# Retention attention and two dense layers on one core: other token blocks for the first layer, another order of the norms in the second

## The chip, the cores and the metric

The program runs on one core of one Trainium2 chip. A core has a matrix engine (TensorE, PE in the profile, with its weight loads shown apart as PEld), a vector engine (VectorE, DVE), a scalar engine (ScalarE, ACT), GpSimd (POOL) and a queue engine that issues the transfers (SyncE, SP). Each engine takes its instructions strictly in the order in which the program lists them, and waits on semaphores where it needs another engine's result. The metric is the device time of one execution in microseconds (us); lower is better.

## What is computed

```python
# attention: q, k, v of (4, 8, 576, 64)
ret = (scale * q @ k.T) * Dmat            # Dmat: gamma**(i-j) below the diagonal, 0 above
x = (ret @ v) -> (2304, 512)              # 2304 tokens, 512 features
# first layer: w_in (512, 2048), w_out (2048, 512)
h = x @ w_in
x = (h * sigmoid(1.702 * h)) @ w_out
# second layer: w_in (512, 1024), w_out (1024, 512)
h = x @ w_in
e = exp(h - max(h)); solu = h * e / (sum(e) + 1e-9)
ln = (solu - mean(solu)) / sqrt(var(solu) + 1e-6) * g_ln
out = ln @ w_out
```

## The kernel before

**Precision.** A float32 product is made of three matmuls on halves: each operand is split into a high part (a rounding copy, cast on ACT or DVE) and a low part (the difference, on POOL or DVE), and the products high-high, low-high and high-low are summed in PSUM. So every logical matmul is three instructions, each with its own weight load.

**First layer.** The 2304 tokens are cut into five blocks (`BLOCKS`): four of 464 tokens and one of 448. The 16 column groups of `w_in` are taken in three generations (`GENS`) of 3, 5 and 8 groups, since the split weights don't all fit. `STEPS` runs over generation, block and group: 80 steps. A step issues 12 matmuls for h (`emit_h`, L442; moving operand as wide as the block) and 12 matmuls for the step before it that add into y (`emit_y`, L472). Between them stands a chain: a sigmoid on ACT (L447), a product on DVE (L448), a cast (L452 on DVE or L450 on ACT) and a subtraction on DVE (L453). `split_x` makes the halves of the next block's x near the end of a block (ACT L422, POOL L423), in pieces that don't cross a sequence's end (every 576 tokens). At a block's end y is copied by ACT (L478, first generation) or added by DVE (L480). In between, `background` slips in pieces of weight preparation (conversions on DVE, L225 to L236; splits on ACT L248 and POOL L253), a set number for each step.

**Second layer.** Its 18 tiles of 128 tokens are taken in 9 pairs. For a pair p, `split_y` makes seven split operands (subtractions on DVE, casts on ACT L507, subtractions on POOL L508). `emit_h2(p)` computes the two tiles' h by a scheme with seven products instead of eight: the products are made in the order B, A, C, A, B, C, D, each of six matmuls (L546), with adds on DVE (L552) and copies on ACT (L555, L558, L564) between them; the fifth product writes over the bank of the first, so it waits for the first add (c12) to have read it. `hooks` are places in `emit_h2` where the caller puts other work into the order.

`norm(t, steps)` is the work on tile t: step 1 is a maximum on DVE (L583) and an exponential on ACT (L584); step 2 is a product u*e on DVE (L586, alone as "u") and then the statistics ("v": L588 to L593 on DVE and a power of one column on POOL, L594); step 3 is the scaling on DVE (L596). `turn(t)` transposes the tile on PE (`emit_T`, L607), and splits the result (ACT L616, DVE L617); it needs step 3. `out(t)` multiplies by `w_out` (L634, 24 matmuls), copies the result (ACT L639) and stores it (SP). After pair 1 the order for a pair is: `emit_h2(p+1)`, `turn(2p)`, `split_y(p+2)`, maxima and exponentials of the new pair, `out(2p-1)`, step 2, `turn(2p+1)`, step 2, `out(2p)`.

Of the kernel before, what the change touches and what calls it, by code (L numbers as in the profile page):

```python
# [10 lines left out]
F32R = mybir.dt.float32r  # L11
# [8 lines left out]
NT = B * S  # L20
DM = H * D
F1 = 2048
F2 = 1024
P = 128
CH = 128
NCH = 4
LAST = S - NCH * CH
TB = 464
NB = -(-NT // TB)
BLOCKS = [(t, min(TB, NT - t)) for t in range(0, NT, TB)]  # L30
NF = F1 // P
FH = NF // 2
GENS = ((0, 3), (3, 8), (8, 16))
# [86 lines left out]
RAW_AT = [_M["att"], _M["att"] + SLICE]  # L120
T_LATER = T_START + [SCAN_AT] + [_M["att"] + (2 + i) * SLICE for i in range(5)]
# [3 lines left out]
E_AT = [RAW_AT[1], T_LATER[4]]  # L125
# [1 line left out]
IDENT_AT = _M["g"]  # L127
STAT_AT = IDENT_AT + P
S_AT = [T_LATER[4], T_LATER[5], T_LATER[4]] + [T_LATER[5]] * 6
E_FIRST = RAW_AT[0]  # L130

# [13 lines left out]
class Build:  # L147
    def __init__(self, tc, ctx, att, consts, ident_in, w1, w2in, w2out, out):
        self.tc, self.nc = tc, tc.nc
        self.att_in, self.const_in, self.ident_in = att, consts, ident_in  # L150
        self.w1_in, self.w2in_in, self.w2out_in, self.out = w1, w2in, w2out, out
        pool = lambda name: ctx.enter_context(tc.tile_pool(name=name, bufs=1))
        self.mem = pool("mem").tile([P, CMEM], F32, name="mem")
        self.wp = pool("wp")
        self.ctx, self.early, self.early_s = ctx, ExitStack(), ExitStack()
        pad = ctx.enter_context(tc.tile_pool(name="pad", bufs=1, side="right"))
        self.pad = pad.tile([P, RIGHT_PAD], F32, name="pad")
        self.gs = self.early_s.enter_context(
            tc.tile_pool(name="gsp", bufs=1, side="right", reuse_waits="tile")
        ).tile([P, 4, 512], F32R, name="gs")  # L160
        self.xp = self.early.enter_context(tc.tile_pool(name="xp", bufs=1, reuse_waits="tile"))
        self.xsp = self.early_s.enter_context(
            tc.tile_pool(name="xsp", bufs=1, side="right", reuse_waits="tile")
        )
        self.xb = self.xp.tile([P, B * NP * S], F32, name="xb")
        self.xst, self.w, self.wraw = {}, {}, {}
        self.ps = ctx.enter_context(tc.tile_pool(name="ps", bufs=1, space=bass.MemoryType.PSUM))
        self.bg, self.split, self.staged = [], set(), set()
# [242 lines left out]
    def split_x(self, gen, j, k):  # L411

        nc = self.nc
        t = self.xsp.tile([P, 2, 512], F32R, tag="xs", name=f"xs{gen}_{j}_{k}", bufs=6)
        self.xst[gen, j, k] = t
        (t0, width), done = BLOCKS[j], 0
        while done < width:
            b, s = divmod(t0 + done, S)
            n = min(width - done, S - s)
            assert (4, b * NP + k) in self.staged  # L420
            x = self.x(b * NP + k)[:, s:s + n]
            nc.scalar.copy(t[:, 0, done:done + n], x)  # L422
            nc.gpsimd.tensor_tensor(  # L423
                t[:, 1, done:done + n], x, f32(t[:, 0, done:done + n]), ALU.subtract
            )
            done += n
# [4 lines left out]
    def emit_h(self, gen, j, f, lo_engine, hi_act=False):  # L431
# [12 lines left out]
        b = BUF[gen, j, f]  # L444
        g = self.at(_M["g"] + b * TB, width)
        gs = self.gs[:, b * 2:b * 2 + 2, 0:width]
# [82 lines left out]
    def emit_h2(self, p, hooks={}):  # L529

        nc = self.nc
        ys = self.xst.pop(p)

        B_, A, C, D_ = (self.ybank(f"h2_{p}_{i}") for i in range(4))
        c11, c12, c21, c22 = (
            self.h(2 * p + i)[:, n * 512:(n + 1) * 512] for i in range(2) for n in range(2)
        )

        def mul(o, a, b, start, stop):
            a = ys[a]  # L540
            i = 0
            hi, lo = self.w[b]
            for k in range(2):
                w = slice(k * 512, (k + 1) * 512)
                for l, m in ((0, hi), (1, hi), (0, lo)):
                    nc.tensor.matmul(  # L546
                        o, a[:, l, k], m[:, w], start=(start and i == 0), stop=(stop and i == 5),
                        skip_group_check=True,
                    )
                    i += 1  # L550

        add = lambda o, a, b: nc.vector.tensor_tensor(o, a, b, ALU.add)  # L552
        mul(B_, "s2", "t2", True, True)
        mul(A, "a11", "b11", True, True)
        nc.scalar.copy(c11, A)  # L555
        add(c12, B_, c11)
        mul(C, "s1", "t1", True, True)
        nc.scalar.copy(c22, C)  # L558
        hooks.get("u2", int)()
        mul(A, "a12", "b21", False, True)  # L560
        mul(B_, "s3", "t3", False, True)
        mul(C, "s4", "b22", False, True)
        add(c21, B_, c11)
        nc.scalar.copy(c11, A)  # L564
        add(c22, c22, c21)
        add(c12, C, c12)
        hooks.get("p3", int)()
        hooks.get("c12", int)()
        mul(D_, "a22", "t4", True, True)
        add(c21, D_, c21)  # L570

    def norm(self, t, *steps):

        nc = self.nc
        u, e = self.h(t), self.at(E_FIRST if t == 1 else E_AT[t % 2], F2)
        st = self.at(STAT_AT + (t % 4) * 32, 32)
        nm, sm, q, v, r = (st[:, i:i + 1] for i in range(5))
        bn = st[:, 6:18].rearrange("r (n s) -> r n s", n=2)  # L580
        mv = st[:, 18:20]
        if 1 in steps:
            nc.vector.reduce_max(nm, u, axis=AX.X, negate=True)  # L583
            nc.scalar.activation(e, u, AF.Exp, bias=nm, accum_out=sm)  # L584
        if 2 in steps or "u" in steps:
            nc.vector.tensor_tensor(u, u, e, ALU.mult)  # L586
        if 2 in steps or "v" in steps:
            nc.vector.tensor_scalar_add(q, sm, 1e-9)  # L588
            nc.vector.tensor_scalar(q, q, q, 1e-6, ALU.mult, ALU.mult)  # L589
            for n in range(2):  # L590
                nc.vector.bn_stats(bn[:, n], u[:, n * 512:(n + 1) * 512])  # L591
            nc.vector.bn_aggr(mv, bn)  # L592
            nc.vector.tensor_tensor(v, mv[:, 1:2], q, ALU.add)  # L593
            nc.gpsimd.tensor_tensor(r, v, self.const("half"), ALU.pow)  # L594
        if 3 in steps:
            nc.vector.tensor_scalar(u, u, mv[:, 0:1], r, ALU.subtract, ALU.mult)  # L596
# [46 lines left out]
    def run(self):  # L643
# [35 lines left out]
        for f in range(FH):  # L679
            t = T_START[f % 2]  # L680
# [7 lines left out]
        last = B * NP - 1  # L688
# [36 lines left out]
        for g, j, f in STEPS:  # L725
            fl, n = f - GENS[g][0], GENS[g][1] - GENS[g][0]
            start = g == 0 and j == 0
# [42 lines left out]
            if g == len(GENS) - 1 and last_block:  # L770
                assert not self.bg
                if fl == 0:
                    self.open_second()
                    ys, y1, y2 = (self.split_y(p) for p in range(3))
# [22 lines left out]
        def turn(t):  # L797
            zs[t] = self.split_z(t, self.emit_T(t))

        def out(t):  # L800
            self.emit_out(t, zs.pop(t))


        last = [
            self.split_weight(NF + i, T_LATER[4 + i], pool) for i, pool in ((2, None), (3, (self.zsp, 1)))
        ]
        def run(pieces):
            for piece in pieces:
                piece()
# [3 lines left out]
        nc.scalar.activation(self.at(STAT_AT, 1), self.const("half"), AF.Exp)  # L813

        self.emit_h2(0, {
            "u2": lambda: run(y1[6:8] + last[1]), "p3": lambda: run(y1[8:]), "c12": lambda: self.norm(0, 1),
        })

        def first():
            self.norm(0, "v")  # L820
            self.norm(0, 3)
            self.norm(1, 1)

        def start():
            turn(0)
            run(y2[4:])
            self.norm(1, 2)

        self.norm(0, "u")
        self.emit_h2(1, {"u2": first, "p3": start})  # L830
        self.norm(1, 3)
        self.norm(2, 1)
        out(0)
        turn(1)
        pairs = NTT // 2
        for p in range(1, pairs):
            more = p + 1 < pairs
            if p == 1:
                self.emit_h2(p + 1, {"u2": lambda: [self.norm(2, 2), self.norm(3, 1), self.norm(2, 3)]})
            elif more:  # L840
                self.emit_h2(p + 1, {"u2": lambda: [self.norm(2 * p + i, 3) for i in range(2)]})
            else:
                self.norm(2 * p, 3)
                self.norm(2 * p + 1, 2, 3)
            turn(2 * p)
            if p == 1:
                self.norm(3, 2, 3)
            if p + 2 < pairs:
                run(self.split_y(p + 2))
            if more:  # L850
                self.norm(2 * p + 2, 1)
                self.norm(2 * p + 3, 1)
            out(2 * p - 1)
            if more:
                self.norm(2 * p + 2, 2)
            turn(2 * p + 1)
            if p + 2 < pairs:
                self.norm(2 * p + 3, 2)
            out(2 * p)
        out(NTT - 1)  # L860
# [74 lines left out]
```

## Time and profile before

| | |
|---|---|
| median of three timed runs | 686.6 us (686.52 to 687.75) |
| the profiled execution's own time | 684.85 us |
| its span, first to last instruction | 683.1 us |
| mean granted TensorE clock | 0.999 |
| busy: PE, DVE, ACT, POOL | 670.5, 491.7, 234.4, 232.0 us |

The rows are of the profiled execution, so sums are made against its 684.85 us, which is 1.75 us over its span and 1.75 us below the median. In the rows, times are from the start of the span. "x12" means that twelve instructions of one kind in a row are merged in a line; the first number is the start of the first of them. What stands in brackets is the idle time of the engine before the line, and what ended it.

### The profile page before, as it was taken

How to read it: one execution, taken by the hardware profiler on the slowest of the kernel's cores; microseconds unless marked ns; L12 is line 12 of the kernel's file. 1: busy time of each engine (PE TensorE's matmuls, PEld its weight loads, DVE VectorE, ACT ScalarE, POOL GpSimd, SP SyncE). 2: the span in 40 equal slices, each digit the busy share in tenths (PEclk: the TensorE clock that was granted, in tenths of full speed). 3: DMA queues.
4: the chain of work that ended last, by engine and by line, in shares of the span. 5: the costliest groups of instructions: out<-in, count | busy, mean ns of one | idle time of the engine just before them, and what ended most of it. 6: DMA issues, size and time to landing. Idle time of an engine off the chain costs nothing. (4 is left out here: it accounts for less than half of the span.)

```text
span 683.1 us, 10367 instructions
## 1 busy us (share of the span) xinstructions
PE 670.5 (98%) x4070; PEld 591.5 (87%) x4070; DVE 491.7 (72%) x805; ACT 234.4 (34%) x483; POOL 232.0 (34%) x240
## 2 busy tenths in 40 slices
PE   8999999999999999999999999999989999999998
PEld 7999888998888899988888888998777788888887
DVE  3899766877887876577676775565779877877780
ACT  3654444442112134111111211456535424453331
POOL 1211366453323248411120301396634314431300
PEclk9999999999999999999999999999999999999999
DMA  8999400002213110012211100000000000000001
GB/s 326 422 383 373 155 0 2 0 1 94 92 63 124 61 62 1 0 63 93 92 63 62 63 1 0 1 1 4 1 15 32 1 31 32 31 17 17 31 32 47
DMA packets 13441, 49.34 MB, mean 72 GB/s; under 512 B 1488, under 2 KB 2384, under 8 KB 11984
## 3 DMA queue, kind: packets, MB, share of 16 engines
q1 hardware_dynamic: 13392, 48.68, 19.5%
q8 instruction: 32, 0.52, 0.3%
q14 instruction: 17, 0.14, 0.1%
HBM read 43.95 MB, written 4.72 MB: 71 GB/s over the span
## 5 line engine op out<-in xcount | busy, mean ns | idle before, releaser
L442 PE MATMUL h<-xs,w 128*128 128x464 f32 (+1 forms) x960 | 213.4, 371 | 0.4 <-POOL xs L423 0.4
L472 PE MATMUL yp<-gs,w 128*128 128x464 f32 (+1 forms) x960 | 212.2, 370 | 0.0
L442 PEld LDWEIGHTS h<-xs,w 128*128 128x128 f32 x960 | 180.1, 188 | 21.0 <-POOL xs L423 2.0
L472 PEld LDWEIGHTS yp<-gs,w 128*128 128x128 f32 x960 | 180.3, 188 | 18.9
L423 POOL TENSOR_TENSOR xs<-xb,xs 128x112 fp32r<-128x112 f32 (+4 forms) x96 | 92.7, 993 | 227.6 <-ACT xs L422 227.6
L447 ACT ACTIVATE mem<-h 128x464 f32<-128x464 f32 (+1 forms) x80 | 44.6, 557 | 263.9 <-PE h L442 246.1
L448 DVE TENSOR_TENSOR mem<-h,mem 128x464 f32<-128x464 f32 (+1 forms) x80 | 51.0, 638 | 95.0 <-ACT mem L447 94.7
L634 PE MATMUL o<-w,zs 128*128 128x512 f32 (+1 forms) x456 | 103.2, 382 | 1.2 <-ACT zs L616 0.9
L634 PEld LDWEIGHTS o<-w,zs 128*128 128x128 f32 x456 | 81.2, 188 | 17.0 <-ACT zs L616 1.4
L253 POOL TENSOR_TENSOR w<-mem,w 128x512 fp32r<-128x512 f32 x40 | 54.2, 1383 | 68.3 <-ACT w L248 68.3
L453 DVE TENSOR_TENSOR gs<-mem,gs 128x464 fp32r<-128x464 f32 (+1 forms) x80 | 66.5, 831 | 13.6 <-ACT gs L450 7.0
L508 POOL TENSOR_TENSOR ys_s<-mem,ys_s 128x256 fp32r<-128x256 f32 x36 | 33.8, 950 | 58.4 <-ACT ys_s L507 58.4
L452 DVE CAST gs<-mem 128x464 fp32r<-128x464 f32 (+1 forms) x69 | 42.0, 608 | 6.6
L546 PE MATMUL h<-wt,ys_s 128*128 128x512 f32 x162 | 41.4, 391 | 0.7 <-DVE mem L552 0.7
L552 DVE TENSOR_TENSOR mem<-h,mem 128x512 f32<-128x512 f32 x36 | 24.7, 687 | 22.1 <-PE h L546 13.5
L546 PEld LDWEIGHTS h<-wt,ys_s 128*128 128x128 f32 x162 | 30.3, 188 | 7.3 <-DVE mem L552 1.2
L422 ACT CAST xs<-xb 128x112 fp32r<-128x112 f32 (+4 forms) x96 | 34.9, 431 | 0.0
L594 POOL TENSOR_TENSOR mem<-mem 128x1 f32<-128x1 f32 x18 | 9.9, 551 | 65.2 <-DVE mem L593 65.2
L617 DVE TENSOR_TENSOR zs<-zT,zs 128x512 fp32r<-128x512 f32 x36 | 23.1, 685 | 9.3 <-ACT zs L616 9.3
L586 DVE TENSOR_TENSOR mem<-mem 128x1024 f32<-128x1024 f32 x18 | 25.4, 1410 | 4.4 <-ACT mem L584 4.4
L546 PE MATMUL h<-wb,ys_a 128*128 128x512 f32 x108 | 27.4, 389 | 0.0
L584 ACT ACTIVATE mem<-mem 128x1024 f32<-128x1024 f32 x18 | 20.6, 1145 | 18.7 <-DVE mem L583 18.7
(80 smaller groups left out, 732.6 us busy)
## 6 DMA issues: line engine op xcount, KB each, us to landing
mem<-in_att SPq DMA_DIRECT2D x11, 1120.0 KB, 8.2
wraw<-in_w SPq DMA_DIRECT2D x16, 512.0 KB, 10.3
mem<-in_w SPq DMA_DIRECT2D x16, 512.0 KB, 3.5
out<-mem SPq DMA_DIRECT2D x17, 256.0 KB, 2.0
mem<-in_w2in SPq DMA_DIRECT2D x8, 512.0 KB, 3.4
mem<-in_w2out SPq DMA_DIRECT2D x8, 512.0 KB, 3.5
mem<-in_att SPq DMA_DIRECT2D x5, 544.0 KB, 8.7
mem<-in_att SPq DMA_DIRECT2D x4, 576.0 KB, 8.7
```

What stands on the lines that cost most here:

```text
L253: nc.gpsimd.tensor_tensor(lo[:, c], w[:, c], f32(hi[:, c]), ALU.subtract)
L422: nc.scalar.copy(t[:, 0, done:done + n], x)
L423: nc.gpsimd.tensor_tensor(t[:, 1, done:done + n], x, f32(t[:, 0, done:done + n]), ALU.subtract)
L442: nc.tensor.matmul(h[:, 0:width], a[:, w], x[:, b, 0:width], start=(n == 0), stop=(n == 3 * KB - 1))
L447: nc.scalar.activation(g, h[:, 0:width], AF.Sigmoid, scale=1.702)
L448: nc.vector.tensor_tensor(g, h[:, 0:width], g, ALU.mult)
L452: nc.vector.tensor_copy(gs[:, 0], g)
L453: lo_engine.tensor_tensor(gs[:, 1], g, f32(gs[:, 0]), ALU.subtract)
L472: nc.tensor.matmul(o, a[:, w], gs[:, b], start=(first and i == 0), stop=(last and i == 2))
L508: nc.gpsimd.tensor_tensor(ys[:, 1], src, f32(ys[:, 0]), ALU.subtract)
L546: nc.tensor.matmul(o, a[:, l, k], m[:, w], start=(start and i == 0), stop=(stop and i == 5), skip_group_check=True,)
L634: nc.tensor.matmul(o[:, 0:n], z[:, a, k], b[:, c:c + n], start=(k == 0 and i == 0), stop=(k == FB - 1 and i == 2),)
```

## The change

The five blocks of the first layer become 384, 512, 512, 512 and 384 tokens wide; the buffers that were `TB` wide follow. The number of blocks, steps and matmuls stays. In the second layer, the maximum and the exponential of a tile can now be issued apart ("max", "exp"), `emit_h2` has two more hook places (`c21`, right after the second add, and `sums`, after the last of the middle adds; `p3` now stands before these adds), and for the tiles 0 to 5 the steps are issued in another order. Tile 3's exponential gets a buffer of its own (`E_FIRST`).

```diff
-TB = 464
-NB = -(-NT // TB)
-BLOCKS = [(t, min(TB, NT - t)) for t in range(0, NT, TB)]
+TB = 512
+WIDTHS = (384, 512, 512, 512, 384)
+NB = len(WIDTHS)
+BLOCKS = [(sum(WIDTHS[:j]), w) for j, w in enumerate(WIDTHS)]
...
-E_FIRST = RAW_AT[0]
+E_FIRST = {1: RAW_AT[0], 3: T_LATER[5]}
...
         mul(C, "s4", "b22", False, True)
+        hooks.get("p3", int)()
         add(c21, B_, c11)
+        hooks.get("c21", int)()
         nc.scalar.copy(c11, A)
         add(c22, c22, c21)
         add(c12, C, c12)
-        hooks.get("p3", int)()
+        hooks.get("sums", int)()
         hooks.get("c12", int)()
...
-        if 1 in steps:
+        if 1 in steps or "max" in steps:
             nc.vector.reduce_max(nm, u, axis=AX.X, negate=True)
+        if 1 in steps or "exp" in steps:
             nc.scalar.activation(e, u, AF.Exp, bias=nm, accum_out=sm)
...
-            "u2": lambda: run(y1[6:8] + last[1]), "p3": lambda: run(y1[8:]), "c12": lambda: self.norm(0, 1),
+            "u2": lambda: run(y1[6:8] + last[1]), "sums": lambda: run(y1[8:]), "c12": lambda: self.norm(0, 1),
...
         def first():
-            self.norm(0, "v")
-            self.norm(0, 3)
-            self.norm(1, 1)
+            self.norm(1, "exp")
+            self.norm(0, "v", 3)
+            self.norm(1, "u")
 
         def start():
             turn(0)
+            self.norm(1, "v")
             run(y2[4:])
-            self.norm(1, 2)
-
+
+        self.norm(1, "max")
         self.norm(0, "u")
-        self.emit_h2(1, {"u2": first, "p3": start})
-        self.norm(1, 3)
+        self.emit_h2(1, {"u2": first, "p3": start, "c21": lambda: self.norm(1, 3)})
         self.norm(2, 1)
+        self.norm(3, "max")
         out(0)
         turn(1)
...
             if p == 1:
-                self.emit_h2(p + 1, {"u2": lambda: [self.norm(2, 2), self.norm(3, 1), self.norm(2, 3)]})
+                self.emit_h2(p + 1, {
+                    "u2": lambda: [self.norm(3, "exp"), self.norm(2, 2)],
+                    "c21": lambda: [self.norm(2, 3), self.norm(3, 2)], "sums": lambda: self.norm(3, 3),
+                })
+            elif p == 2:
+                self.emit_h2(p + 1, {"u2": lambda: [self.norm(4, 3), self.norm(5, 2, 3)]})
...
             turn(2 * p)
-            if p == 1:
-                self.norm(3, 2, 3)
...
             turn(2 * p + 1)
-            if p + 2 < pairs:
+            if 1 < p < pairs - 2:
                 self.norm(2 * p + 3, 2)
```

## Rows read from the trace of the kernel before

**Rows 1.** The page's busy times: us, share of the span, instructions.
```profile
PE 670.5 (98%) x4070; PEld 591.5 (87%) x4070; DVE 491.7 (72%) x805; ACT 234.4 (34%) x483; POOL 232.0 (34%) x240
```

**Rows 2.** Groups by line and shape, TensorE: busy us, mean ns of one.
```profile
L442 PE MATMUL h<-xs,w 128*128 128x464 f32 x768 | 171.9, 372 | 0.4 <-POOL xs L423 0.4
...
L442 PE MATMUL h<-xs,w 128*128 128x448 f32 x192 | 41.5, 365 | 0.0
```

**Rows 3.** Timeline of the first layer: start, us, engine, line; PE groups of h.
```profile
325.64 2.67 PE L442 MATMUL h<-xs,w 128*128 128x464 f32 x12
...
345.69 2.67 PE L442 MATMUL h<-xs,w 128*128 128x464 f32 x12
...
441.00 2.59 PE L442 MATMUL h<-xs,w 128*128 128x448 f32 x12
...
462.88 2.60 PE L472 MATMUL yp<-gs,w 128*128 128x448 f32 x12
```

**Rows 4.** The chain that ended last, in order of time: start, us, what.
```profile
594.83 9.52 PE h L546 x42
...
668.71 11.25 PE o L634 x72
```

**Rows 5.** Timeline of the second layer's first pairs, TensorE alone.
```profile
491.20 1.64 PE L546 MATMUL h<-wt,ys_a 128*128 128x512 f32 x6
...
493.77 0.50 PE L634 MATMUL o<-w,zs 128*128 128x512 f32 x1 [0.93 <-ACT zs L616]
...
494.50 5.48 PE L634 MATMUL o<-w,zs 128*128 128x512 f32 x23 [0.22 <-DVE zs L617]
...
501.89 1.09 PE L607 MATMUL zT<-mem 128*128 128x128 f32 x8 [1.91 <-DVE mem L596]
...
513.17 5.73 PE L634 MATMUL o<-w,zs 128*128 128x512 f32 x24
...
520.60 1.06 PE L607 MATMUL zT<-mem 128*128 128x128 f32 x8 [1.70 <-DVE mem L596]
...
526.97 1.52 PE L546 MATMUL h<-wt,ys_s 128*128 128x512 f32 x6
...
533.32 1.66 PE L546 MATMUL h<-wt,ys_s 128*128 128x512 f32 x6 [0.74 <-DVE mem L552]
```

**Rows 6.** The same stretch: VectorE, ScalarE and GpSimd around the norms.
```profile
482.10 1.22 DVE L583 TENSOR_REDUCE mem<-mem 128x1 f32<-128x1024 f32 x1
...
484.62 1.65 DVE L586 TENSOR_TENSOR mem<-mem 128x1024 f32<-128x1024 f32 x1 [0.71 <-ACT mem L584]
...
486.80 0.14 DVE L588 TENSOR_SCALAR mem<-mem 128x1 f32<-128x1 f32 x1
...
489.48 0.81 DVE L596 TENSOR_SCALAR mem<-mem 128x1024 f32<-128x1024 f32 x1 [0.67 <-POOL mem L594]
...
500.43 0.56 POOL L594 TENSOR_TENSOR mem<-mem 128x1 f32<-128x1 f32 x1
...
503.06 1.16 ACT L584 ACTIVATE mem<-mem 128x1024 f32<-128x1024 f32 x1 [6.71 <-DVE mem L583]
...
505.29 1.29 DVE L617 TENSOR_TENSOR zs<-zT,zs 128x512 fp32r<-128x512 f32 x2 [2.33 <-ACT zs L616]
...
532.58 0.68 DVE L552 TENSOR_TENSOR mem<-h,mem 128x512 f32<-128x512 f32 x1
```

**Rows 7.** Timeline of the first layer's last block, VectorE.
```profile
456.10 2.93 DVE L487 TENSOR_TENSOR mem<-mem 128x512 f32<-128x512 f32 x2
...
461.64 0.63 DVE L453 TENSOR_TENSOR gs<-mem,gs 128x448 fp32r<-128x448 f32 x1 [0.64 <-ACT gs L450]
```

**Rows 8.** Timeline of the second block's first step: POOL's splits, PE's wait.
```profile
85.02 2.92 POOL L423 TENSOR_TENSOR xs<-xb,xs 128x112 fp32r<-128x112 f32 x4 [6.48 <-ACT xs L422]
...
87.99 0.48 PE L442 MATMUL h<-xs,w 128*128 128x464 f32 x1 [0.37 <-POOL xs L423]
```

**Rows 9.** Busy time of each engine in one stretch of the first layer.
```profile
170.00:290.00 120.00, 120.00 (x579) 108.37 (x579) 90.80 (x131) 29.86 (x57) 48.52 (x43) 1.00 0.18 57
```

More of the change, by code (lines that the diff above doesn't have):

```diff
@@ L159, in __init__ @@
             tc.tile_pool(name="gsp", bufs=1, side="right", reuse_waits="tile")
-        ).tile([P, 4, 512], F32R, name="gs")
+        ).tile([P, 4, TB], F32R, name="gs")
         self.xp = self.early.enter_context(tc.tile_pool(name="xp", bufs=1, reuse_waits="tile"))
@@ L413, in split_x @@
         nc = self.nc
-        t = self.xsp.tile([P, 2, 512], F32R, tag="xs", name=f"xs{gen}_{j}_{k}", bufs=6)
+        t = self.xsp.tile([P, 2, TB], F32R, tag="xs", name=f"xs{gen}_{j}_{k}", bufs=6)
         self.xst[gen, j, k] = t
@@ L576, in norm @@
         nc = self.nc
-        u, e = self.h(t), self.at(E_FIRST if t == 1 else E_AT[t % 2], F2)
+        u, e = self.h(t), self.at(E_FIRST.get(t, E_AT[t % 2]), F2)
         st = self.at(STAT_AT + (t % 4) * 32, 32)
```

## The prediction

> **What bounds the kernel now.** I read the page's busy times first: PE works through 98% of the span [rows 1], DVE through 72%. So PE sets the time, and only two things can move it: the time from one matmul's start to the next, and PE's idle time. Next came the chain that ended last. From 533 us to the end it holds PE alone, but for the last copy and store (in rows 4 two of its links), so whatever PE gains before that point arrives at the end whole. Then the timeline. In the first layer PE's groups follow one another without idle time, but for rare waits as in rows 8. In the second layer's first pairs five PE groups start late [rows 5]; later pairs show none of it.
>
> How far apart matmuls start is read from the starts of groups, since the mean of one [rows 2] is a latency that overlaps the next. 464 wide: 8 groups of 12 lie between 325.64 and 345.69, so 20.05 / 96 = 208.9 ns. 448 wide: 9 groups between 441.00 and 462.88 give 21.88 / 108 = 202.6 ns [rows 3]. 512 wide: 9.52 / 42 = 226.7 ns [rows 4]. 256 wide: the last 72 matmuls are 24 of 512 and 48 of 256 columns, so (11.25 - 24 x 0.2267) / 48 = 121 ns [rows 4]. The clock is at its upper level, 2.4 GHz (1.00 in rows 9), at which the columns alone take 193.3, 186.7, 213.3 and 106.7 ns. What comes on top is 15.6, 15.9, 13.4 and 14 ns. It isn't the same at all widths: 512 and 256 columns pay about 13.5, 464 and 448 nearly 16.
>
> **The widths.** The first layer has 1536 matmuls of 464 columns and 384 of 448 (rows 2 for h; y has as many): 1536 x 0.2089 + 384 x 0.2026 = 320.9 + 77.8 = 398.7 us. After: 1152 of 512 and 768 of 384. For 512, I take 226.7 ns: it is the same width, though measured in the other layer. 384 isn't in the trace. Its columns take 160.0 ns; from below it adds 13.3 ns (as 512), from above 15.9 (as 448). I take 13.3, so 173.3 ns, since 384 is like 512 and 256 a whole number of 128 columns, which 464 and 448 are not; that this is what counts is a guess. Sum: 261.2 + 133.1 = 394.3, **4.4 us less**. With the upper end for 384 it is 396.3, 2.4 less. With about 15.7 ns for every width nothing changes, as the columns and the number of matmuls stay.
>
> The Trainium skill ("TensorE: Matmul & The Clock Gate", Back-to-back issue gap) gives a warm gap of N / 2.4 + 2.5 ns, an overhead that doesn't know the width. The rows disagree with its size (226.7 where it gives 215.8) and with its being constant; by it, the widths would give nothing.
>
> What the widths may cost. A step of 384 takes 24 x 0.1733 = 4.16 us instead of 5.01, and work that has no width must fit in it.
> - The second block's first h waits 0.37 us for POOL's split of x [rows 8]. The new block is 512 wide: its four pieces take 2.92 x 512/464 = 3.22, 0.3 more, while PE gets there about 0.2 sooner and the chain ahead of the split is as much shorter. +0.3 us.
> - In the last block, all of POOL's weight splits go on at the old pace and stretch DVE: two subtractions of 512 columns take 2.93 us [rows 7] where such an add takes 0.68 [rows 6]. There the low half of g is ready at 461.64 + 0.63 = 462.27 for a y group at 462.88 [rows 3]: 0.6 us to spare. The time from the end of h to that y group is one step's, and shrinks by 24 x (0.2026 - 0.1733) = 0.7, the DVE chain itself by 0.1 to 0.2 at most, so part of the step waits, and the next one may. I take +0.7 us for this block.
> - DVE as a whole: 90.80 of 120 us [rows 9], 3.8 us in a step of 5.01. Even if none of it shrank it would fit in 4.16.
> Together **+1.0 us**, from 0.2 to 2.5. The number of x pieces stays (8 for each generation and quarter of x, before and after), and no transfer is added or moved past another.
>
> **The norms.** What PE loses now, by starts [rows 5] and 226.7 ns for a matmul: 491.20 + 6 x 0.2267 = 492.56 to 493.77, 1.21; 494.00 to 494.50, 0.50; 494.50 + 23 x 0.2267 = 499.71 to 501.89, 2.18; 513.17 + 24 x 0.2267 = 518.61 to 520.60, 1.99; 526.97 + 24 x 0.2267 = 532.41 to 533.32, 0.91. Sum 6.8; about 0.2 of it are joints between kinds of groups that stay. **6.6 us can be won.**
>
> Now the new order, on the old time axis, with these durations [rows 6]: maximum 1.2; product u*e 1.2, or 1.65 beside POOL's splits; statistics from their first instruction to the scaling 486.80 to 489.48, 2.7 (0.7 of it waiting for POOL); scaling 0.8; an add 0.68; both z subtractions 1.3.
> - Tile 0: tile 1's maximum now stands ahead of its product, but the product waited 0.71 us for the exponential anyway, so it moves from 484.62 to about 485.0, and the first transposes from 490.35 to about 490.7. **+0.35 us**, new. Behind it the add c12 ends at 487.3, and the fifth product of the pair, which overwrites what it reads, starts at 487.6.
> - The first output group waited for ACT's cast, which stood behind tile 1's exponential and a copy. The exponential now runs before the transposes, the copy after. With 0.87 us for eight transposes the cast can start near 491.4, and z is there before the D product ends at 493.0. The 1.21 and 0.50 go.
> - Tile 1's power on POOL stood behind the seven splits of y2, and ran at 500.43. It is now listed ahead of them; they follow from 495.9 to about 501, still before the pair that uses the last of them (507). From tile 0's scaling at 489.8 DVE has: 0.8, product 1.2, z 1.3 (a little later, on the cast), statistics 2.7 with an add inside the wait. Tile 1 is scaled at 495.9 to 496.7; PE needs it after 24 output matmuls, at 498.5. The 2.18 goes, with 1.8 to spare.
> - Tile 2: three adds and the maximum end at 499.8, and its exponential starts. In the old trace the same series on ACT (exponential, copy of the output, casts) and the z subtractions took from 503.06 to 506.58, 3.5 us, so 503.3 here. Then add 0.68, product 1.2, statistics 2.7, scaling 0.8: 508.7. PE is through with transposes and the seven products (0.87 + 9.52 from 498.5) at 508.9. This is the tightest place: 0.2 us.
> - Tile 3: product, statistics (two adds inside or behind the wait), scaling, to about 513.6. PE asks at 508.9 + 0.87 + 5.46 = 515.3. The 1.99 goes.
> - Tile 5's product and statistics leave the place ahead of the add c12 of pair 3. Before that add DVE now has an add, z, four subtractions for the next pair (under 0.7 each), two maxima, tile 4's product and statistics, z: about 12 us from 513.6, so c12 ends near 526.3. The fifth product asks at 521.7 + 5.5 = 527.2. The 0.91 goes, with 0.9 to spare.
> - From there the order is the old one, DVE about 2 us later against PE than now, with idle time of its own to catch up.
> Of the 6.6 I take 0.35 for tile 0 and 0.45 for the tight places: **-5.8 us**, between -3.5 and -6.5.
>
> **Rivals.**
> 1. *384 columns pay 15.9 ns.* For it: 448 is the nearest width. 768 x 2.6 ns is 2.0 us less gain: 679.4 us.
> 2. *All matmuls of the first layer pay about 15.7 ns, whatever the width.* For it: both layers differ in which operand moves, and 512 and 256 are seen in the second layer alone. The widths give nothing: 677.4 + 4.4 = 681.8 us. The rule of the Trainium skill quoted above would come to this too.
> 3. *The norms' waits move on instead of going.* The margins for tile 2 and for the two adds are 0.2 to 0.9 us; if ACT's series comes 1 us later at each of them, three waits of about 1 us come back: 680.4 us.
> 4. *Slower: DVE can't hold the 384-wide steps.* There are 32 of them. To lose the 9.2 us won and 1.4 more, each must overrun by 0.33 us, so that DVE needs 4.5 us in a step instead of the 3.8 of a wider step now. Only stretching by POOL, as in rows 7, could do it, and POOL is busy 40% there [rows 9]. 688 us or more.
>
> **The numbers.** -4.4 + 1.0 - 5.8 = -9.2 us. On the profiled execution 684.85 - 9.2 = 675.65; that execution lies 1.75 below the median, so the median after is **677.4 us**. Chances: this forecast 0.56, rival 1 0.16, rival 2 0.14, rival 3 0.09, rival 4 0.03, something else 0.02. The likeliest case with its own bounds (tile waits, last block) goes from 675.5 (-4.4 + 0.2 - 6.5, and 0.4 for the spread of the runs) to 679. The range reaches on to rivals 1 to 3: **675.5 to 682.5**, which takes in rival 2 with its spread. A change under 0.2%, 1.4 us, is about what a measurement of this kernel can't tell from none. Faster than 685.2: the first four cases, less a little for several costs at once, 0.92; same 0.04; slower 0.04.
>
> **What the profile after would show.** Groups of 12 matmuls of 512 columns start 2.72 us apart in the first layer and those of 384 2.08 us (rival 1: 2.11; rival 2: 2.75 and 2.11). The first layer's last y group ends about 3.4 us sooner. In the second layer the transposes of tiles 1 and 3 have no wait before them, POOL's second power stands before y2's splits, and the fourth pair's products start about 8.3 us sooner. Wrong would be: waits of PE for L453 in each 384-wide step, PE waits for L596 or L552 between 490 and 530 that sum to over 3 us, or a constant overhead in the spacings.

## The result and the profile after

The kernel after takes 676.41 us (median of 5 runs, 676.09 to 676.72) against 686.52 before (5 runs, 685.57 to 687.75): ratio 0.985, 95% interval 0.9831 to 0.9868. The forecast was 677.4 us, -9.2; measured -10.1. The profiled execution of after has a time of its own of 676.72 us and a span of 674.8, so between the two profiled executions 8.1 us are gone (8.3 of the span).

The page's busy times, to be read beside [rows 1]:

```profile
PE 666.7 (99%) x4070; PEld 580.0 (86%) x4070; DVE 494.4 (73%) x805; ACT 233.2 (35%) x483; POOL 235.8 (35%) x240
```

The same 4070 matmuls, so what went is time between them. A cut at two starts of PE splits the span: the first layer from its first h (70.06 us before, 70.39 after) to the first product of the second layer (472.62 and 470.59), and the rest. First layer: 402.6 to 400.2, -2.4. Rest: 210.46 to 204.24, -6.2. Ahead of the first layer +0.3.

The first layer's groups of 12, by the timeline after (start, us, engine, line; the answer to [rows 3]):

```profile
425.76 2.88 PE L473 MATMUL yp<-gs,w 128*128 128x512 f32 x12
...
431.20 2.88 PE L473 MATMUL yp<-gs,w 128*128 128x512 f32 x12
...
442.97 2.24 PE L443 MATMUL h<-xs,w 128*128 128x384 f32 x12
...
459.61 2.24 PE L443 MATMUL h<-xs,w 128*128 128x384 f32 x12
```

Two groups of 512 columns in 5.44 us are 226.7 ns for a matmul; eight groups of 384 in 16.64 us are 173.3 ns. Both are the values that the sum took, to the last digit, where no block's end is near.

The second layer's first pairs, by the timeline after (in brackets the idle time and what ended it; to be read beside [rows 5, 6]). Lines moved: L586 is the maximum, L588 the exponential, L590 the product u*e, L598 POOL's power, L600 the scaling, L611 the transposes, L553 the adds.

```profile
487.27 0.81 DVE L600 TENSOR_SCALAR mem<-mem 128x1024 f32<-128x1024 f32 x1 [0.67 <-POOL mem L598]
...
488.32 1.03 PE L611 MATMUL zT<-mem 128*128 128x128 f32 x8
...
490.58 5.63 PE L638 MATMUL o<-w,zs 128*128 128x512 f32 x24
...
492.88 0.55 POOL L598 TENSOR_TENSOR mem<-mem 128x1 f32<-128x1 f32 x1 [5.65 <-DVE mem L597]
493.40 0.74 POOL L509 TENSOR_TENSOR ys_s<-mem,ys_s 128x256 fp32r<-128x256 f32 x1
493.47 1.22 DVE L600 TENSOR_SCALAR mem<-mem 128x1024 f32<-128x1024 f32 x1
...
496.05 1.04 PE L611 MATMUL zT<-mem 128*128 128x128 f32 x8
...
501.42 1.65 PE L547 MATMUL h<-wb,ys_a 128*128 128x512 f32 x6 [0.25 <-ACT mem L556]
...
506.06 0.81 DVE L600 TENSOR_SCALAR mem<-mem 128x1024 f32<-128x1024 f32 x1
...
507.02 1.07 PE L611 MATMUL zT<-mem 128*128 128x128 f32 x8
...
511.07 0.80 DVE L600 TENSOR_SCALAR mem<-mem 128x1024 f32<-128x1024 f32 x1
...
513.40 1.04 PE L611 MATMUL zT<-mem 128*128 128x128 f32 x8
...
519.76 1.52 PE L547 MATMUL h<-wt,ys_s 128*128 128x512 f32 x6
```

The four lines of transposes have no bracket: PE doesn't stand idle ahead of them. The power of tile 1 stands ahead of the splits (L509) now. The fourth pair's products start at 519.76 instead of 526.97, 7.2 us sooner (8.3 were forecast). One wait is left, and it is a new one: the fourth product group of the third pair, at 501.42, waits for ACT's copy (L556).

What the first layer gave back: two places of the timeline after, the second block's first step (to be read beside [rows 8]) and the last y group.

```profile
86.48 0.50 PE L443 MATMUL h<-xs,w 128*128 128x512 f32 x1 [0.41 <-POOL xs L424]
...
465.82 1.51 DVE L518 TENSOR_TENSOR mem<-mem 128x256 f32<-128x256 f32 x1
...
467.25 0.55 DVE L449 TENSOR_TENSOR mem<-h,mem 128x384 f32<-128x384 f32 x1
...
468.39 2.36 PE L473 MATMUL yp<-gs,w 128*128 128x384 f32 x12 [0.29 <-ACT gs L451]
```

The last block's last product with the sigmoid (L449) stands behind a sum of 256 columns, which took 1.51 us while POOL made splits (L518 and L512 are the sums and differences that `split_y` makes on VectorE; all are called sums below). Its wait and the one behind it come to 0.57 us by PE's starts.

A smaller cost stands in no bracket. Where a block ends, and most of all where the width changes with it, some matmuls of a group start a few ns late each. The next two groups, one of the old width and one of the new, start 2.77 us apart, where a 512-wide group above takes 2.72:

```profile
436.02 2.92 PE L473 MATMUL yp<-gs,w 128*128 128x512 f32 x12
...
438.79 2.27 PE L443 MATMUL h<-xs,w 128*128 128x384 f32 x12
```

Over the first layer such small delays sum to 0.9 us (before: 0.1), 0.6 of it in the 24 groups beside a change of width. Why they occur isn't shown.

### The profile page after: what moved, and what is told of

The parts are those of the page before. It is cut to its first block, busy times and chain, and to the rows that moved or that the text cites. A ratio compares the mean times of both kernels' runs of the same rounds, so it can differ in the third digit from the quotient of the medians.

```text
span 674.8 us, 10368 instructions
## 1 busy us (share of the span) xinstructions
PE 666.7 (99%) x4070; PEld 580.0 (86%) x4070; DVE 494.4 (73%) x805; ACT 233.2 (35%) x483; POOL 235.8 (35%) x240
## 4 chain that ended last, share of the span: by engine, by line
PE 86%; DVE 7%; issue 2%; ACT 2%; DMA 1%; POOL 0%; SPq 0%; DVEq 0%; POOLq 0%; ACTq 0%
PE h L443 28%; PE yp L473 28%; PE o L638 14%; PE h L547 10%; PE zT L611 2%; PE o L384 2%; PE s L351 1%; PE o L372 1%; DMA mem<-in_att 1%; DVE mem L331 1%; DVE mem L355 1%; DVE mem L553 1%; DVE mem L449 1%; DVE mem L586 1%; ACT gs L451 1%
## 5 line engine op out<-in xcount | busy, mean ns | idle before, releaser
L443 PE MATMUL h<-xs,w 128*128 128x512 f32 (+1 forms) x960 | 211.7, 368 | 0.4 <-POOL xs L424 0.4
L473 PE MATMUL yp<-gs,w 128*128 128x512 f32 (+1 forms) x960 | 211.0, 368 | 0.3 <-ACT gs L451 0.3
L473 PEld LDWEIGHTS yp<-gs,w 128*128 128x128 f32 x960 | 174.9, 188 | 23.9 <-DVE mem L481 0.7
L424 POOL TENSOR_TENSOR xs<-xb,xs 128x384 fp32r<-128x384 f32 (+3 forms) x96 | 95.2, 1018 | 228.1 <-ACT xs L423 228.1
L448 ACT ACTIVATE mem<-h 128x512 f32<-128x512 f32 (+1 forms) x80 | 44.5, 556 | 263.9 <-PE h L443 259.4
L449 DVE TENSOR_TENSOR mem<-h,mem 128x512 f32<-128x512 f32 (+1 forms) x80 | 50.9, 636 | 89.5 <-ACT mem L448 89.3
L454 DVE TENSOR_TENSOR gs<-mem,gs 128x512 fp32r<-128x512 f32 (+1 forms) x80 | 68.1, 851 | 13.0 <-ACT gs L451 6.4
L509 POOL TENSOR_TENSOR ys_s<-mem,ys_s 128x256 fp32r<-128x256 f32 x36 | 35.0, 983 | 51.9 <-ACT ys_s L508 41.8
L453 DVE CAST gs<-mem 128x512 fp32r<-128x512 f32 (+1 forms) x69 | 39.9, 578 | 6.6
L547 PE MATMUL h<-wt,ys_s 128*128 128x512 f32 x162 | 41.3, 390 | 0.0
L553 DVE TENSOR_TENSOR mem<-h,mem 128x512 f32<-128x512 f32 x36 | 24.5, 686 | 21.2 <-PE h L547 12.5
L547 PEld LDWEIGHTS h<-wt,ys_s 128*128 128x128 f32 x162 | 30.3, 188 | 6.2
L423 ACT CAST xs<-xb 128x384 fp32r<-128x384 f32 (+3 forms) x96 | 35.0, 433 | 0.0
L598 POOL TENSOR_TENSOR mem<-mem 128x1 f32<-128x1 f32 x18 | 10.3, 574 | 64.7 <-DVE mem L597 64.7
L547 PE MATMUL h<-wb,ys_a 128*128 128x512 f32 x108 | 27.6, 390 | 0.2 <-ACT mem L556 0.2
L590 DVE TENSOR_TENSOR mem<-mem 128x1024 f32<-128x1024 f32 x18 | 24.7, 1373 | 3.7 <-ACT mem L588 3.7
L232 DVE SCALAR_TENSOR_TENSOR mem<-mem 128x512 uint32<-128x512 uint32 x32 | 26.7, 833 | 0.6
```

The lines of the kernel that those rows point to most:

```text
L424: nc.gpsimd.tensor_tensor(t[:, 1, done:done + n], x, f32(t[:, 0, done:done + n]), ALU.subtract)
L443: nc.tensor.matmul(h[:, 0:width], a[:, w], x[:, b, 0:width], start=(n == 0), stop=(n == 3 * KB - 1))
L448: nc.scalar.activation(g, h[:, 0:width], AF.Sigmoid, scale=1.702)
L449: nc.vector.tensor_tensor(g, h[:, 0:width], g, ALU.mult)
L453: nc.vector.tensor_copy(gs[:, 0], g)
L454: lo_engine.tensor_tensor(gs[:, 1], g, f32(gs[:, 0]), ALU.subtract)
```

## The experiments

All runs in one table; e3, e4 and e11 were timed once, so they have no interval and serve for reading spacings alone. "First layer" and "rest" are cut as above, from the profiled execution; the ratio is that of the timed runs to runs of the kernel before on the same chip, with its 95% interval.

| run | first layer, us | rest, us | span, us | median, us | ratio |
|---|---|---|---|---|---|
| before | 402.6 | 210.5 | 683.1 | 686.5 | 1 |
| after | 400.2 | 204.2 | 674.8 | 676.41 | 0.985 (0.9831 to 0.9868) |
| e1 widths alone | 400.3 | 211.7 | 681.9 | 683.22 | 0.9944 (0.9929 to 0.9958) |
| e2 order alone | 404.2 | 204.3 | 679.1 | 680.94 | 0.991 (0.9896 to 0.9924) |
| e3 widths, multiples of 16 | 403.7 | 204.2 | 678.6 | 680.34 (one run) | |
| e4 widths, multiples of 8 | 405.0 | 204.2 | 679.0 | 680.89 (one run) | |
| e5 power first | 404.0 | 208.6 | 683.2 | 684.91 | 0.9968 (0.9959 to 0.9977) |
| e6 tile 5 back | 400.3 | 205.8 | 676.4 | 677.96 | 0.9875 (0.9861 to 0.989) |
| e7 narrow first | 401.7 | 204.7 | 676.5 | 678.35 | 0.9881 (0.9864 to 0.9897) |
| e8 narrow last | 399.0 | 204.2 | 673.7 | 675.27 | 0.9835 (0.9821 to 0.985) |
| e9 and sum moved | 399.5 | 204.7 | 674.8 | 676.46 | 0.9843 (0.9826 to 0.9861) |
| e10 after again | 400.1 | 204.2 | 675.1 | 676.36 | 0.984 (0.9822 to 0.9857) |
| e11 more widths | 408.7 | 204.6 | 684.0 | 685.73 (one run) | |
| e12 all sums late | 398.4 | 205.2 | 673.6 | 675.91 | 0.9836 (0.9823 to 0.985) |

**Each half of the change alone.** The widths without the new order, in the kernel before:

```diff
-TB = 464
...
+TB = 512
+WIDTHS = (384, 512, 512, 512, 384)
...
```

> The kernel before with the new block widths alone. My theory: the widths and the norms are two savings that add up; matmuls of 512 columns start 226.7 ns and those of 384 columns 173.3 ns apart also here, which takes 4.4 us, and new waits in the first layer give some 2.1 back; the five late groups of the second layer stay at 6.8 us. Span near 680.8 us, ratio near 0.997. Rival: the widths cause the loss of the waits too, since the second layer's first pairs find VectorE at another phase; then the span falls to 678 us or less. Second rival: without the new order the saving of the widths is eaten by longer waits in the second layer; span near 683.

And the new order on the old blocks, in the kernel after:

```diff
-TB = 512
-WIDTHS = (384, 512, 512, 512, 384)
...
+TB = 464
...
```

> The new order of the norms alone, on blocks of 464 and 448 tokens. My theory: the first layer is that of before (402.5 us from its first h to the second layer's first product), and the second layer loses its 6.2 us of late groups: span near 676.9 us, ratio near 0.991. Rival: part of the 6.2 us came from the widths; then the second layer keeps waits of over 1 us and the span is 678 us or more.

The order alone brings the rest of the span to 204.3 us, as in the kernel after; the widths alone leave it at 211.7, and bring the first layer to 400.3, as in the kernel after. In time the ratios add up: 0.56% and 0.9%, against 1.5%. So the two halves are separate savings, and the first rival of the first run falls, and that of the second (its span is over 678 us, but by the first layer). Two sizes are off, though. The rest is 211.7 in the first run, not 210.5, so over half of the 2.3 us saved in the first layer was lost again. That is near the size of the second rival, but the waits in the second layer didn't grow. The timeline shows what did (the lines stand one further than before: L608 are the transposes, L547 the products, L597 the scaling):

```profile
499.25 1.09 PE L608 MATMUL zT<-mem 128*128 128x128 f32 x8 [1.89 <-DVE mem L597]
500.10 2.61 PE L547 MATMUL h<-wt,ys_s 128*128 128x512 f32 x6
502.51 2.18 PE L547 MATMUL h<-wb,ys_a 128*128 128x512 f32 x6
504.53 1.52 PE L547 MATMUL h<-wt,ys_s 128*128 128x512 f32 x6
```

Six matmuls take 2.41 us from 500.10 and 1.36 us from 504.53 on. The table of windows of the same run gives the granted clock (the third number from the end): 0.63 right after the waits, 1.00 before and later.

```profile
497.00:499.00 2.00, 0.36 (x2) 0.00 (x0) 0.62 (x1) 0.00 (x0) 1.35 (x3) 1.00 0.00 0
499.30:503.80 4.50, 4.50 (x18) 3.71 (x19) 2.17 (x3) 2.69 (x5) 0.00 (x0) 0.63 0.15 58
504.00:506.00 2.00, 2.00 (x10) 1.63 (x10) 0.65 (x2) 0.59 (x1) 0.00 (x0) 1.00 0.00 0
```

After PE's idle waits of 0.80, 0.23 and 1.89 us between 490 and 499, the clock fell to its lower level, 1.2 GHz, for a while. The profiled execution of before has nearly the same waits (0.93, 0.22 and 1.91 us, [rows 5]) and keeps its clock, so it isn't shown that the waits brought the fall. What the fall cost is shown: the two slowed groups took 2.41 + 2.02 us, 1.6 more than the same two before (1.47 and 1.36). Waits that were 0.3 us shorter in all gave part of it back. In the 40 timed runs of before on the experiments' four chips, the eight over 687.9 us all have a mean granted clock of 0.998 or less, which fits such a fall; the one of e1's five at 1.000 (682.85 us) lies among the others (682.53 to 684.28), which doesn't. All ten timed runs of the kernel after, e10 included, have 1.000.

The other size: in the second run the first layer takes 404.2 us, 1.7 more than the same blocks before. Its timeline:

```profile
302.10 2.68 PE L442 MATMUL h<-xs,w 128*128 128x464 f32 x12
...
347.46 2.68 PE L442 MATMUL h<-xs,w 128*128 128x464 f32 x12
```

18 groups in 45.36 us: 210.0 ns for 464 columns, where [rows 3] gave 208.9. The e5 run, with the old widths too, has 404.0, and shows both spacings in one execution:

```profile
163.97 2.67 PE L472 MATMUL yp<-gs,w 128*128 128x464 f32 x12
...
194.05 2.67 PE L472 MATMUL yp<-gs,w 128*128 128x464 f32 x12
...
304.45 2.68 PE L472 MATMUL yp<-gs,w 128*128 128x464 f32 x12
...
334.69 2.68 PE L472 MATMUL yp<-gs,w 128*128 128x464 f32 x12
```

12 groups in 30.08 us are 208.9 ns for a matmul, 12 in 30.24 are 210.0. In the first stretch the starts of single matmuls lie 207 to 210 ns apart; in the second they are 205 and 215 ns apart in turn. In before, e2 and e5 either pattern holds through a block, often through several, and changes only where one block ends and the next begins; what decides between them isn't shown. So the spacing at 464 isn't a constant, not even of one execution; over the first layer it moves the time by up to 1.7 us. At 512 and 384 columns all of after, e1, e6 and e10 lie within 400.1 and 400.3 us.

**One wait of the norms at a time.** In the kernel before, tile 1's statistics ahead of the splits that stood before them on POOL:

```diff
             turn(0)
-            run(y2[4:])
             self.norm(1, 2)
+            run(y2[4:])
```

> The kernel before with one swap: tile 1's product and statistics are listed ahead of the splits of the third pair, so that GpSimd's power no longer stands behind seven subtractions. My theory: the wait of 2.18 us ahead of tile 1's transposes is two thirds GpSimd's queue: the power runs at 498.6 instead of 500.4, and the transposes start 1.6 to 1.9 us sooner; the other late groups stay. Span near 681.4 us. Rival: VectorE's chain alone sets that start (maximum, adds, product, statistics); then the power moves and nothing else, under 0.3 us.

The rest of the span falls from 210.5 to 208.6 us, -1.9, by the one swap. The power runs at 500.15 instead of 500.43 on an axis that lies 2.0 us later (first output matmul at 495.73, before at 493.77), so 2.2 us sooner, and PE no longer stands idle ahead of the transposes:

```profile
500.15 0.55 POOL L594 TENSOR_TENSOR mem<-mem 128x1 f32<-128x1 f32 x1 [8.75 <-DVE mem L593]
...
500.74 1.22 DVE L596 TENSOR_SCALAR mem<-mem 128x1024 f32<-128x1024 f32 x1
...
502.01 1.09 PE L607 MATMUL zT<-mem 128*128 128x128 f32 x8
```

So 1.85 of the 2.18 us went with POOL's queue. By starts 0.34 us are left (the output matmuls would let the transposes start at 501.67): the scaling, L596, ends at 501.96, as it took 1.22 us beside POOL's splits instead of 0.81. DVE's chain ahead of the power became only 0.3 us shorter: the product u*e, with no splits beside it now, took 1.22 us instead of 1.45. The span stays at 683.2 because in this execution the first layer took 1.5 us longer than before, the 404.0 of above, and the part ahead of it 0.5 us; the timed ratio, 0.9968, shows the gain.

In the kernel after, tile 5's product and statistics at their old place, ahead of the add c12:

```diff
-self.emit_h2(p + 1, {"u2": lambda: [self.norm(4, 3), self.norm(5, 2, 3)]})
+self.emit_h2(p + 1, {"u2": lambda: [self.norm(4, 3), self.norm(5, 3)]})
...
-            if 1 < p < pairs - 2:
+            if p < pairs - 2:
                 self.norm(2 * p + 3, 2)
```

> The kernel after with tile 5's product and statistics back at their old place, ahead of the add c12 of the fourth pair. My theory: c12 ends some 3 us later, 1.9 us after the fifth product asks for its bank, so PE loses 1.3 to 2.0 us there and nothing elsewhere; span near 676.5 us. Rival: the new order of the earlier tiles leaves VectorE far enough ahead that the old place costs nothing; span 674.8 us as after.

```profile
522.81 1.22 DVE L590 TENSOR_TENSOR mem<-mem 128x1024 f32<-128x1024 f32 x1
...
525.89 0.68 DVE L553 TENSOR_TENSOR mem<-h,mem 128x512 f32<-128x512 f32 x1
...
526.63 1.67 PE L547 MATMUL h<-wt,ys_s 128*128 128x512 f32 x6 [1.26 <-DVE mem L553]
```

Product and statistics (from 522.81) stand ahead of the add at 525.89, and the fifth product waits for it. The rest grows by 1.6 us, the first layer stays. The place costs what was said; the rival falls.

**Which widths are dear.** Blocks of other widths, in the kernel after, to read the spacing:

```diff
-WIDTHS = (384, 512, 512, 512, 384)
+WIDTHS = (416, 480, 496, 432, 480)
```

> The kernel after with blocks of 416, 480, 496, 432 and 480 tokens, to read the start-to-start time of a matmul at each width. Theory A (only whole multiples of 128 columns are cheap): every one of these widths pays about 15.6 to 16 ns over its columns: 416 189.2, 432 195.8, 480 215.8, 496 222.5 ns. Theory B (the overhead falls smoothly towards 512): 496 13.9, 480 14.6, 432 16.5, 416 17 ns. Theory C (a multiple of 32 is enough, and 448 was special): 416 and 480 pay 13.3, 432 and 496 nearly 16. With A the span is about 4 us over that of the kernel after.

```diff
+WIDTHS = (320, 488, 504, 504, 488)
```

> The same reading with blocks of 320, 488, 504, 504 and 488 tokens: multiples of 8 that aren't multiples of 16, and 320, two and a half times 128. Theory A: 320 149.3, 488 219.2, 504 225.8 ns, all with about 15.9 ns over their columns. Theory B: 504 13.6, 488 14.3, 320 over 17. Theory C: 320 pays 13.3, 488 and 504 nearly 16.

```diff
+WIDTHS = (400, 472, 456, 488, 488)
```

> The kernel after with blocks of 400, 472, 456, 488 and 488 tokens, for the start-to-start time at more widths. Theory D, after the two earlier readings: the columns count as rounded up to 16, and a fixed 13.3 ns comes on top, except that widths from 416 to 496 which are whole multiples of 16 pay some 2 to 3 ns more: 488 220.0, 472 213.3, 456 206.7 ns; 400 either 180.0 (if cheap like 384) or 182.5. Theory E: the extra belongs to a range of widths and not to the rounding; then 472 and 456 lie 2 ns or more higher, near 216 and 209, and only 488 and 504 are free of it.

From starts of groups of 12 without waits, as above (columns at 2.4 GHz subtracted):

| columns | ns, start to start | over the columns |
|---|---|---|
| 320 | 146.7 | 13.3 |
| 384 | 173.3 | 13.3 |
| 400 | 180.0 | 13.3 |
| 416 | 188.3 | 15.0 |
| 432 | 195.8 | 15.8 |
| 448 | 202.6, also 206.7 in e2 | 15.9, 20.0 |
| 456 | 208.9 | 18.9 |
| 464 | 208.9, also 210.0 in e2 and e5 | 15.6, 16.7 |
| 472, 480, 496, 504 | 213.3, 216.7, 223.3, 226.7 | 16.7 |
| 488 | 220.0 in e4, 225.7 in e11 | 16.7, 22.4 |
| 512 | 226.7 | 13.3 |

Two pairs of lines for it, from e4 (10 groups of 320 in 17.60 us, 5 of 488 in 13.20):

```profile
255.20 2.80 PE L443 MATMUL h<-xs,w 128*128 128x488 f32 x12
...
268.40 2.80 PE L473 MATMUL yp<-gs,w 128*128 128x488 f32 x12
...
281.19 1.92 PE L473 MATMUL yp<-gs,w 128*128 128x320 f32 x12
...
298.79 1.92 PE L473 MATMUL yp<-gs,w 128*128 128x320 f32 x12
```

No theory came through. Theory A, which was the guess behind the forecast's 173.3 ns, falls with 320 and 400, which are cheap and no multiples of 128. B falls with 504, dearer than 400. C falls with 416 and 480. D, which was drawn up with e4's 488 in hand, fits 400 and 472 in e11 and misses 456 and 488 there; E fits 456 and misses 472 and 488. What the runs show: 13.3 ns at 512 and at 320 to 400, and 15 to 22 ns from 416 to 504, where the same width can differ between kernels, between executions and within one. The cause stays open. The spans (678.6, 679.0 and 684.0 us) follow the spacings, with e11 the worst.

**The waits that the widths brought.** The order of the blocks alone, in the kernel after:

```diff
-WIDTHS = (384, 512, 512, 512, 384)
+WIDTHS = (384, 384, 512, 512, 512)
```

> The kernel after with blocks of 384, 384, 512, 512 and 512 tokens. My theory of the waits that the widths brought (some 2.1 us): a narrow block ahead of a wide one leaves GpSimd's last split late (0.69 us in the first generation, 0.27 in each of the others), and the last block's steps of 4.16 us leave VectorE late for the last y group (0.57 us). Here the last block is wide, so the last 0.57 goes, and the first of the narrow-to-wide steps moves from block 0 to block 1; span 674.0 to 674.5 us. Rival: the waits have to do with the number of narrow steps, not their place; span as after, 674.8.

```diff
+WIDTHS = (512, 512, 512, 384, 384)
```

> The kernel after with blocks of 512, 512, 512, 384 and 384 tokens. My theory: a narrow block is followed by a wide one only where a generation changes, with a whole step more for the split, so the waits of 0.27 us shrink and the first one is that of a wide pair, about as before; the wait ahead of the last y group stays (0.57 us) and may grow, since the block ahead of the last is narrow too. Span 674.3 to 675. Rival: two narrow blocks in a row let VectorE fall behind at the generations' ends; span 676 or more.

The first misses: 401.7 us instead of under 400. The wait ahead of the last y group did go, but two narrow blocks in a row at the start leave POOL further behind: its eight subtractions for the third block end 1.15 us late. The rest is 0.4 us longer too: tile 0's transposes start that much later after the layer's first product.

```profile
92.55 7.56 POOL L424 TENSOR_TENSOR xs<-xb,xs 128x384 fp32r<-128x384 f32 x8
...
100.17 0.50 PE L443 MATMUL h<-xs,w 128*128 128x512 f32 x1 [1.15 <-POOL xs L424]
```

So it isn't the number of narrow steps, which is the same, but where a wide block follows narrow ones. The second bears that out: the narrow blocks at the end give 399.0 us, 1.2 less than after, and the wait ahead of the last y group stays. The span, 673.7 us, is somewhat under what was expected.

That wait was tried too, on the blocks of the run before (512, 512, 512, 384 and 384), together with a run of the kernel after on the same chip:

```diff
-6: y1[3:4] + y2[0:1], 7: y2[1:3] + y1[4:6],
+6: y1[3:4], 7: y2[0:3] + y1[4:6],
```

> Blocks of 512, 512, 512, 384 and 384 tokens, and the first sum for the third pair's split moved from the last block's seventh step to its eighth. My theory: the wait ahead of the last y group (0.57 us with either order of the blocks) came from VectorE, where two additions of 256 columns stretched to 1.5 us each stood ahead of the last product with the sigmoid; without one of them that product starts 1.4 us sooner and the wait goes: 0.4 to 0.6 us under the same blocks without the move, span near 673.2, and 1.4 to 1.7 us under the kernel after. Rival: the move only shifts VectorE's work to where the second layer's first products wait for it, no gain over the blocks alone.

> The kernel after once more, beside the run above on the same chip. First layer 400.2 us, second layer 200.8 us, span 674.3 to 674.9 us. If the gain of the other order of blocks is only a difference of chips, the two runs agree within 0.5 us.

The wait went, as expected, and came back a step later: the sums, 1.86 us for two beside POOL's splits, now stand ahead of the additions that free the y banks.

```profile
467.74 1.86 DVE L512 TENSOR_TENSOR mem<-mem 128x256 f32<-128x256 f32 x2
...
469.52 1.94 DVE L481 TENSOR_TENSOR mem<-yp,mem 128x384 f32<-128x384 f32 x4
...
470.12 1.65 PE L547 MATMUL h<-wt,ys_s 128*128 128x512 f32 x6 [0.90 <-DVE mem L481]
```

The rival had it: with 676.46 us the run isn't faster than the kernel after on the same chip, 676.36. The last attempt, on the same blocks, puts all four sums behind those additions (in the diff, the last lines follow the last y group):

```diff
-7: y2[1:3] + y1[4:6],
+7: y1[4:6],
...
-        y2[3]()
+        for p in y2[0:4]:
+            p()
```

> Blocks of 512, 512, 512, 384 and 384 tokens, and all four sums of the third pair's split put behind the last y additions instead of in front of them. My theory: in the run with the sums in the last step, VectorE was late for the additions that free the y banks; behind them it sits idle for 1.9 us anyway until the first add of the second layer. So the last y group and the first products both start without a wait, 0.5 us under the blocks alone: first layer 398.4 to 398.6 us, span 673.1 to 673.6. Rival: four sums take longer than that idle time and the waits move into the second layer, span 673.7 or more.

The first layer is down to 398.4 us as expected, and the rest up by 1.0: three sums take 3.71 us there and the add c12 comes at 473.60, late for the fifth product. That costs 0.7 us; tile 0's transposes, 0.3 us later once more, make up the other part.

```profile
469.97 3.71 DVE L512 TENSOR_TENSOR mem<-mem 128x256 f32<-128x256 f32 x3
473.60 0.68 DVE L553 TENSOR_TENSOR mem<-h,mem 128x512 f32<-128x512 f32 x1
...
474.33 1.66 PE L547 MATMUL h<-wt,ys_s 128*128 128x512 f32 x6 [0.35 <-DVE mem L553]
```

Again the rival. Narrow blocks last (e8) has the lowest median, 675.27 us; but the interval of its ratio overlaps that of the kernel after, so that it is faster is shown only for the profiled first layer.

## Why the prediction was right

Point by point, by its own steps:

- **What bounds the kernel.** Right: PE's gain ahead of 533 us arrived whole. From the fourth pair's sixth product to the last output matmuls every group of PE starts 6.22 us sooner after the layer's first product than before.
- **The widths, -4.4 us.** The spacings came out as taken, 226.7 and 173.3 ns, so against the profiled execution of before the term is right to the digit; rivals 1 and 2 are refuted by the rows above. The reason given for 384 (a whole number of 128 columns) was a guess, and wrong, as 320 and 400 show. The value before was that of one execution: others pay 1.5 to 1.7 us more at 464 and 448 columns, as e2 and e5 do. That probably is most of the difference between the 8.1 us of the two profiles and the 10.1 of the medians; the spacing in the timed runs wasn't seen. With rival 2 falls, for these matmuls, the warm gap of N / 2.4 + 2.5 ns that the prediction quoted from the Trainium skill ("TensorE: Matmul & The Clock Gate", Back-to-back issue gap): 226.7 ns were measured at 512 columns where it gives 215.8. That section calls it the gap of an isolated matmul, and here each matmul has a weight load of its own.
- **The waits of the narrow steps, +1.0 us.** The two places named were right, but the term was mis-sized, as it held only these two. Matmuls and waits together: 402.6 - 398.7 = 3.9 us beyond the spacings before, 400.2 - 394.3 = 5.9 after, so +2.0, within the bounds given. The named places cost less than said: the last block 0.57 where 0.7 was taken (0.46 and 0.11 by PE's starts), the second block 0.05 more than before where 0.3 was. Not foreseen: 0.27 us at the second block of each later generation (GpSimd's split again), 0.5 at the third generation's first y groups, whose banks are freed late by VectorE's additions, and 0.8 more than before of small delays at the ends of blocks, most where the width changes. Some small waits of before, about 0.4 us net, went in turn.
- **The norms, -5.8 us.** Measured -6.2. Every wait named went, and e5 and e6 show two of them one by one. The +0.35 us for tile 0 didn't come: its product started only 0.24 us later, and took 1.22 us, not 1.65. Splits on POOL ran beside it in both kernels; before, it started inside one, after, 0.1 us ahead of one. Why that is worth 0.4 us isn't shown. Tile 2 was rightly named the tightest place: scaled at 506.87, asked for at 507.02, 0.15 us to spare where 0.2 was said. Missed was the third pair's fourth product, which waits for ACT's copy behind tile 2's exponential and the casts of tile 1 (0.4 us, and 0.1 behind it); the step had looked at the fifth product alone. That is all that came of rival 3.
- **Rival 4, slower.** VectorE held the 384-wide steps. It was stretched (a sum of 256 columns in 1.51 us, 0.4 alone), but PE waited for it in two of the 32 only: the third generation's first y groups and the last one.
- **The signs given.** Spacings, transposes and POOL's power came as listed. The last y group ended about 2.0 us sooner instead of 3.4 and the fourth pair started 7.2 us sooner instead of 8.3, mostly by the 1.0 us that the first layer gave back beyond what was taken.

By measured sizes against the profiled execution: -4.4 + 2.0 - 6.2 + 0.3 ahead of the first layer = -8.3, the 8.3 of the span. The forecast of -9.2 lies between the -8.1 of the profiles and the -10.1 of the medians. That it is so near the medians is partly luck: 1.0 us too little for the waits stood against an execution of before that was probably some 1.5 us cheaper in its spacings than the timed ones.

## What to carry to other kernels

Read the time between starts of matmuls, not their mean duration, for each width that a trace has: at the same number of matmuls and columns, blocks of 512 and 384 columns beat even ones of 464. When a matmul waits for a chain over several engines, look at what else stands in each engine's queue ahead of the chain's short links: a power of one column behind seven subtractions cost 1.85 us, and a swap of two lines took it away. And a queue at its limit gives a moved instruction's cost back one wait later, as the sums here did twice.

## What the runs showed of the hardware that was not expected

- What a matmul takes over its columns depends on the width: 13.3 ns at 320, 384, 400 and 512 columns, 15 to 22 ns from 416 to 504, and there not even the same within one execution (208.9 and 210.0 ns at 464 in e5, the second with starts 205 and 215 ns apart in turn).
- In the kernel after, the 24 groups of matmuls beside a change between 384 and 512 columns took 0.6 us more in small delays; in the kernel before, the 20 groups beside a change between 464 and 448 took under 0.05.
- Waits of 0.80, 0.23 and 1.89 us within 9 us were followed by a stretch of 4.5 us at a mean granted clock of 0.63 in e1, and in the profiled execution of before, with waits of 0.93, 0.22 and 1.91 us, by none.
